# Moving five branch prefetch hints from the last five units of a kernel to a place ahead of its third batch

## The chip, the cores and the metric

The kernel runs on one core of one Trainium2 chip. The metric is the device time of one execution in microseconds, as the median over several runs. A hardware profile of one execution stands beside it: for every instruction its engine, start and duration, the semaphores it waits for, and every DMA packet with its queue. The core has five engines that each run a stream of instructions of their own: PE (matrix products), DVE (vector), ACT (activation), POOL (general) and SP (which here issues DMAs and closes the program). Their instructions themselves arrive by DMA, in packets that the profile counts under the kind "instruction".

## What is computed

An attention over 8 batches of 8 heads, with 576 tokens and 16 beacon keys of width 64, feeds a low-rank mixer over the tokens and a two-layer network over the channels:

```python
k_all = np.concatenate([beacon_k, k], axis=2)            # 16 + 576 keys
v_all = np.concatenate([beacon_v, v], axis=2)
scores = (q @ k_all.transpose(0, 1, 3, 2)) / sqrt(64)    # causal over the 576 tokens
a = softmax(scores)
x = (a @ v_all).transpose(0, 2, 1, 3).reshape(8, 576, 512)
h = x.transpose(0, 2, 1) @ U @ V                         # rank 32, over the tokens
u = x + h.transpose(0, 2, 1)
out = u + maximum(u @ w_ch1, 0) @ w_ch2                  # 512 -> 2048 -> 512
```

## The kernel before

The work is one unrolled program with no loop on its main path. A pair of heads is a visit (32 in all, four a batch): scores (L410), exponentials on ACT (L419), masks on DVE (L349), the product with the values (L428) and the division by the row sums (L436, L437). After a batch's four visits its mixer runs, and the tokens of all batches are then taken in nine blocks of 512 through the two layers. These blocks are cut into "units", small functions in a list named `queue`, and `fill(n)` runs the next n of them between pieces of the attention, so that PE always has something to do. The order of all five engines is written out by hand (`manual_schedule`): a line of code that comes earlier stands earlier in each engine's stream.

The main path takes exponentials without subtracting the row's maximum. At the end it tests whether any row sum left a safe range: `guard` and `guard_sum` put one number into `badi`, and `values_load` reads it into a register of every engine (L1577). If the number is not zero, a general path computes everything again in a loop over the batches (`with tc.If(n_bad != 0, label="general")`, L1631). For the data here it is zero, and every engine jumps over the general path to the end of the program. The jump is one compare-and-branch an engine, in the profile under L1631. The program's closing semaphores stand under L1676.

A branch can be announced by a hint instruction, one an engine. `tc.mark_branch_hint_location("general", engines=[...])` puts the five hints where it is called, inside a `tc.block()`, and each names the engine's own branch at the label "general". In the profile they are `BRANCH_PREFETCH_HINT` at L1676.

```python
        fill(len(queue) - 8)
        n_bad = nc.values_load(badi[0:1, 0:1], min_val=0, max_val=P)
        fill(len(queue) - HINT)                     # HINT = 5
        with tc.block():
            tc.mark_branch_hint_location("general", engines=[ENG.PE, ENG.Activation, ENG.DVE, ENG.SP, ENG.Pool])
            fill(len(queue))
            hold_back()
```

`hold_back` is a short chain of one-element operations (DVE L1106, ACT L1107, DVE L1108, PE L1110, ACT L1112) that keeps PE, ACT and DVE from the branch until DVE's last addition is done. Ahead of it stand the last additions of the output (L849), the products that they wait for (L909) and the stores of the last block (L858, on SP and ACT).

The third batch is the first one whose visits the loop `for p in range(NP1, NP)` plays. Ahead of that loop the second batch's mixer and its units run, with the regrouping of the third batch's keys and queries on DVE (L292, L294), their transposes on PE (L299), and second-layer products of the first block (L1053).

Of the kernel before, what the change touches and what calls it, by code (L numbers as in the profile page):

```python
# [16 lines left out]
ENG = mybir.EngineType  # L17
# [13 lines left out]
def kernel(  # L31
# [75 lines left out]
    def pst(shape, dtype, name):  # L107

        b = emptied.pop(0)
        t = psum.tile(shape, dtype, tag=f"bank{b}", name=name)  # L110
        bank_of[id(t)] = (b, t)
        return t

    def emptying(t):
        emptied.append(bank_of.pop(id(t))[0])
# [465 lines left out]
    def quad_tiles(q):  # L581

        if q == 0:
            w = [pairs.tile([P, 512], F16, name=f"lw{k}", tag=f"pr{k % 2}") for k in range(4)]
        else:
            w = [staged[q - 1][:, ds(512 * k, 512)] for k in range(4)]
            f = staged[q + 1][:, 0 : 2048].bitcast(F32).rearrange("p (k i x) -> p k i x", k=2, i=2)
            lq["k", q] = (f[:, 0], f[:, 1], f[:, 0])
        lq["w", q] = [x.rearrange("p (c f) -> p c f", c=2) for x in w]
# [17 lines left out]
    def quad_weights(q):  # L607

        def part(c0, d):
            return w1[:, ds(c0, 2), ds(P * d, 2 * P)]  # L610

        a11, a12, a21, a22 = part(0, 2 * q), part(2, 2 * q), part(0, HF + 2 * q), part(2, HF + 2 * q)
        s1, s2, s3, s4 = lq["w", q]
        return [
            lambda o=o, x=x, y=y, op=op: nc.gpsimd.tensor_tensor(out=o, in0=x, in1=y, op=op)
            for o, x, y, op in (
                (s1, a21, a22, ALU.add), (s2, s1, a11, ALU.subtract),
                (s3, a11, a21, ALU.subtract), (s4, a12, s2, ALU.subtract),
            )
        ]  # L620
# [483 lines left out]
    def hold_back():  # L1104

        nc.vector.tensor_copy(out=bad[0:1, :], in_=ones[0:1, :])  # L1106
        nc.scalar.activation(out=warm[0:1, :], in_=bad[0:1, :], func=AF.Copy)  # L1107
        nc.vector.tensor_copy(out=bad[0:1, :], in_=warm[0:1, :])  # L1108
        bps = pst([1, 1], F32, name="bps")
        nc.tensor.matmul(bps, bad[0:1, :], ones[0:1, :], start=True, stop=True)  # L1110
        emptying(bps)
        nc.scalar.activation(out=warm[0:1, :], in_=bad[0:1, :], func=AF.Copy)  # L1112
# [7 lines left out]
    def load_batch(b):  # L1120
        if b < DT0:
            Ls[b] = qk_tiles(b)
            emit_loads(b, Ls[b], vss[b % 2])
        else:
            coming.append(lambda: v_beacon(beacon_v[b], vss[b % 2]))
            coming.extend(lambda j=j: v_tokens(v[b], vss[b % 2], ALLH, [j]) for j in range(NT))

    def load_whole(b):

        Ls[b] = qk_tiles(b)  # L1130
        for i, (src, m) in enumerate(((k[b], nk), (q[b], nq))):
            dst = Ls[b][1][i]
            if i == 0:
                coming.append(lambda d=dst: beacon_load(nc.gpsimd, beacon_k[b], d[:, 0, :, :], ALLH))
            for j in range(NT):
                coming.append(lambda d=dst, s=src, a=m[j] - nq[j], n=m[j], j=j: nc.gpsimd.dma_start(  # L1136
                    out=d[a:n, j, :, :], in_=s[:, ds(q0[j], nq[j]), :].rearrange("h p d -> p h d")
                ))
# [6 lines left out]
    def turns(b):  # L1145

        all_coming()
        new_qT(b)
        kn, qn = Ls[b][1]

        def keys(j0, n):
            nc.sync.dma_start_transpose(
                out=kTs[b % 2].rearrange("p c (j x) -> p (c j) x", x=P)[:, NH2 * j0 : NH2 * (j0 + n), 0 : nk[j0]],
                in_=kn[: nk[j0], j0 : j0 + n, :, :].rearrange("p j h d -> p (j h d)"),
            )

        def queries(j):
            nc.sync.dma_start_transpose(
                out=qTs[b][:, :, ds(q0[j], nq[j])], in_=qn[: nq[j], j, :, :].rearrange("p h d -> p (h d)")
            )  # L1160

        return [lambda: keys(0, NT - 1)] + [lambda j=j: queries(j) for j in range(NT)] + [lambda: keys(NT - 1, 1)]
# [54 lines left out]
    def qkT_of(p):  # L1217
        b, c = divmod(p, NH2)
        new_qT_of(p)
        copies = [(act_copy, nc.vector.tensor_copy) if p == 0 else (nc.vector.tensor_copy,)] * 2  # L1220
        if p in ACT_KEYS:
            copies[0] = (act_copy,)
        if p == NP1:
            copies[1] = (act_copy,)
        turns = by_heads(Ls[b][0], c)
        for i, t in enumerate(prs.get(p, ())):
            if t is not None:
                turns[i] = in_pair(prs[p])[i]
        return qkT_units(turns, qTs[b], kTs[b % 2], c, copies, Ls[0][0][0] if p == 0 else None)
# [11 lines left out]
    def av_of(p):  # L1241
        b, c = divmod(p, NH2)
        if c == 0:
            assert not coming or b < DT0
            xbs[b] = xbp.tile([P, NT, DM], F16, name="xb", tag="xb")
        return [
            lambda i=i: av_unit(b, 2 * c + i, expts_of(p)[i], vss[b % 2], xbs[b]) for i in range(2)
        ]
# [7 lines left out]

    DT0 = 4
    LAG = 10
    HINT = 5
    FAST = 1  # L1260
    PARTS = {3: 1, 4: 1, 5: 1, 6: 3, 7: 3, 8: 3}
    AHEAD = 10
# [8 lines left out]
    queue = []  # L1271
    state = {"t": 0}

    def fill_turns(tr, n):
        for u in tr[:n]:
            u()
        del tr[:n]

    def fill(n):
        while n > 0 and queue:  # L1280
            u = queue.pop(0)
            if u is not None:
                u()
            for x in storing:
                x[0] -= 1
            while storing and storing[0][0] < 0:
                storing.pop(0)[1]()
            if coming:
                coming.pop(0)()
            n -= 1  # L1290
# [46 lines left out]
    def play(line):  # L1337

        for word in line.split():
            what, p = word[0], int(word[1:].split(":")[0] or 0)  # L1340
            if what == "f":
                fill(1)
            elif what in "qk":
                qkT_of(p)["qk".index(what)]()
            elif what == "r":
                regroup_of(p)
            elif what in "ab":
                if what == "a":
                    avs[p] = av_of(p)
                avs[p]["ab".index(what)]()  # L1350
            elif what in "mno":
                units = scores_of(p)
                units[2]() if what == "m" else units[3]("no".index(what))
            elif what == "e":
                scores_of(p)[int(word[-1]) // 2]()
            elif what == "v":
                visit([(int(x[: x.index(":")]), int(g)) for x in word[1:].split(",") for g in x[x.index(":") + 1 :]])

    with tc.manual_schedule(engines={ENG.PE, ENG.Activation, ENG.DVE, ENG.SP, ENG.Pool}):
# [111 lines left out]
        def turn_x(b):  # L1471
            turn, head, parts = mix_units(xbs[b], S * b)
            turn()
            later_mix[:] = [head] + parts

        def mix_between(b):

            mixing[:] = later_mix
            feed(b)
# [69 lines left out]
        )  # L1549

        for p in range(NP1, NP):
            b, c = divmod(p, NH2)
            if c == (1 if b >= DT0 else 0) and b + 1 < B:
                load_batch(b + 1)
            if p == P6 + 3:
                quad_tiles(0)
                coming.extend(quad_weights(0))
            if c == (1 if b + 1 == DT0 else 2) and DT0 <= b + 2 < B:
                load_whole(b + 2)
            qk = qkT_of(p + 2) if P6 <= p and p + 2 < min(NP, DT0 * NH2) else []  # L1560
            if p == P6:
                turn_x(b - 1)
                mix_between(b - 1)
            if c == 0 and DT0 <= b + 1 < B:
                tr = turns(b + 1)
                fill_turns(tr, len(tr))
            if p < P6:
                play(third[c])
            else:
                long_slot(p, c, av_of(p), qk or [lambda: None] * 2)  # L1570
# [4 lines left out]
        queue.insert(len(queue) - 14, guard_sum)  # L1575
        fill(len(queue) - 8)
        n_bad = nc.values_load(badi[0:1, 0:1], min_val=0, max_val=P)  # L1577
        fill(len(queue) - HINT)
        with tc.block():
            tc.mark_branch_hint_location("general", engines=[ENG.PE, ENG.Activation, ENG.DVE, ENG.SP, ENG.Pool])  # L1580
            fill(len(queue))
            hold_back()


    def safe_head(h, qT, kT, vs, xb):
# [95 lines left out]
```

## Time and profile before

| what | value |
| --- | --- |
| time, median of 3 runs | 333.34 us (333.2 to 333.98) |
| the profiled execution's own time | 333.34 us |
| its span, first to last instruction | 331.6 us |
| busy share of the span | PE 97%, PEld (weight loads) 69%, DVE 80%, ACT 59%, POOL 50% |
| granted PE clock | 1.000 |
| packets of instructions | q8: 30 (0.49 MB), q14: 19 (0.16 MB) |

In the profile's rows a `q` behind an engine's name (DVEq, PEldq) means its sequencer: branches, semaphore waits and hints, which are not counted as busy. A row such as `x14: 17/28/2051` gives a count and the shortest, median and longest duration in ns. The chain of work goes back from the last instruction that did work, at each step to what released it.

### The profile page before, as it was taken

The page shows a single profiled execution, that of the slowest core. Times are in us where ns is not written, and L with a number is a line of the kernel's source. Part 1 is how long each engine was busy: PE and PEld are TensorE (multiplying, and loading weights), DVE is VectorE, ACT ScalarE, POOL GpSimd, SP SyncE. Part 2 cuts the span into 40 slices and gives each one's busy share as a digit, 9 for nine tenths or more (in the row PEclk, how much of TensorE's full clock was granted, in tenths as well). Part 3 has the DMA queues.
Part 4 walks back from the last instruction along what each step waited for, and adds up shares of the span by engine and source line. Part 5 has one row for each costly group of instructions (what it writes and reads, how often), then busy time and mean ns, then how long its engine had stood idle before and what let it go on. Part 6 is the DMA issues. An engine that isn't in the chain of part 4 may idle for free.

```text
span 331.6 us, 9286 instructions
## 1 busy us (share of the span) xinstructions
PE 323.0 (97%) x3661; PEld 228.2 (69%) x3661; DVE 264.2 (80%) x610; ACT 196.9 (59%) x432; POOL 166.8 (50%) x263
## 2 busy tenths in 40 slices
PE   7899999999999999999999999999999999999993
PEld 3564555555578656876688888764887888788783
DVE  6676988668998668786878777877788898798993
ACT  5967961689972677348844795479536614704700
POOL 8976744658238960689058923940283036030030
PEclk9999999999999999999999999999999999999999
DMA  8999999999999996899999998995014313305003
GB/s 167 136 165 148 176 187 201 195 193 160 98 129 166 213 133 105 101 171 135 152 149 165 153 135 135 114 203 87 4 65 129 62 43 113 51 30 163 3 30 104
DMA packets 150561, 41.99 MB, mean 127 GB/s; under 512 B 131312, under 2 KB 149936, under 8 KB 150512
## 3 DMA queue, kind: packets, MB, share of 16 engines
q0 software_dynamic: 87568, 18.18, 72.6%
q1 hardware_dynamic: 62144, 22.41, 36.8%
q10 hardware_dynamic: 800, 0.75, 0.7%
q8 instruction: 30, 0.49, 0.6%
q14 instruction: 19, 0.16, 0.2%
HBM read 37.45 MB, written 9.44 MB: 141 GB/s over the span
## 4 chain that ended last, share of the span: by engine, by line
PE 92%; ACT 4%; DMA 2%; DVE 1%; ACTq 0%; issue 0%
PE gps L675 21%; PE po L428 9%; PE mpsA L909 9%; PE qpsA L701 6%; PE mpsD L829 6%; PE sps L410 6%; PE cps L1053 4%; PE gps L1027 4%; PE mpsE L829 3%; PE mpsC L829 3%; PE mpsB L829 3%; PE qpsD L701 3%; PE mpsF L829 2%; ACT expt L377 2%; ACT w L377 2%; PE tps L299 2%
## 5 line engine op out<-in xcount | busy, mean ns | idle before, releaser
L577 POOL TENSOR_TENSOR ob<-ob,ut 128x128 f32<-128x128 f32 x104 | 50.0, 511 | 121.7 <-DVE ob L849 59.4
L419 ACT ACTIVATE expt<-sps 128x496 f16<-128x496 f32 (+2 forms) x192 | 82.0, 542 | 41.8 <-PE sps L410 41.8
L675 PE MATMUL gps<-uT,w 128*128 128x512 f16 (+1 forms) x368 | 78.1, 352 | 0.0
L829 PEld LDWEIGHTS <-gT 128*128 128x128 f16 x576 | 54.3, 98 | 8.7 <-issue 2.6
L675 PEld LDWEIGHTS <-w 128*128 128x128 f16 x368 | 33.2, 98 | 25.6 <-issue 1.6
L653 DVE TENSOR_TENSOR gT<-gT 128x1024 f16<-128x1024 f16 (+3 forms) x87 | 47.0, 561 | 0.9
L683 ACT ACTIVATE gT<-gps 128x512 f16<-128x512 f32 x63 | 37.5, 619 | 16.1 <-PE gps L675 11.9
L239 POOL DMA_DIRECT2D vs<-in_v_dram x50 | 40.0, 811 | 13.9 <-DMA w<-in_moe_w_ch_dram 10.8
L428 PEld LDWEIGHTS <-expt 128*128 128x128 f16 x900 | 33.9, 98 | 8.4 <-issue 1.5
L428 PE MATMUL po<-vs,expt 128*128 128x65 f16 x900 | 36.4, 194 | 0.6 <-DVE expt L349 0.4
L909 PEld LDWEIGHTS <-gT 128*128 128x128 f16 x336 | 31.1, 98 | 4.0
L437 DVE TENSOR_TENSOR xb<-po,rec 128x320 f16<-128x320 f32 x64 | 31.4, 491 | 2.2
L349 DVE TENSOR_TENSOR expt<-expt,bigmask 128x768 f16<-128x768 f16 x56 | 31.3, 598 | 0.4 <-ACT expt L419 0.2
L720 ACT ACTIVATE kept<-qpsA 128x512 f32<-128x512 f32 x18 | 10.9, 603 | 24.1 <-PE qpsA L701 13.2
L410 PE MATMUL sps<-qT,kT 64*128 64x80 f16 (+4 forms) x288 | 22.6, 281 | 0.0
L436 DVE RECIPROCAL rec<-po 128x5 f32<-128x5 f32 x64 | 11.9, 186 | 12.8 <-PE po L428 12.5
L377 ACT ACTIVATE expt<-sps 128x496 f16<-128x496 f32 (+2 forms) x48 | 20.7, 589 | 0.7 <-PE sps L371 0.6
L909 PE MATMUL mpsA<-w,gT 128*128 128x256 f16 x160 | 19.1, 273 | 0.0
L410 PEld LDWEIGHTS <-kT 64*128 64x128 f16 x288 | 10.2, 94 | 12.8 <-issue 8.2
L681 DVE TENSOR_SCALAR gT<-gps 128x512 f16<-128x512 f32 x17 | 11.7, 689 | 8.8 <-PE gps L675 8.6
L1136 POOL DMA_DIRECT2D st<-in_k_dram x20 | 16.9, 860 | 1.3 <-DVE pr L294 1.3
L1136 POOL DMA_DIRECT2D st<-in_q_dram x20 | 16.9, 869 | 1.0 <-DMA st<-in_k_dram 0.5
(165 smaller groups left out, 540.4 us busy)
## 6 DMA issues: line engine op xcount, KB each, us to landing
out_dram<-ob SPq DMA_DIRECT2D x33, 256.0 KB, 3.2
vs<-in_v_dram POOLq DMA_DIRECT2D x18, 128.0 KB, 7.0
w<-in_moe_w_ch_dram POOLq DMA_DIRECT2D x4, 512.0 KB, 7.1
w<-in_moe_w_ch_dram POOLq DMA_DIRECT2D x2, 1024.0 KB, 12.2
st<-in_k_dram POOLq DMA_DIRECT2D x12, 128.0 KB, 6.2
st<-in_q_dram POOLq DMA_DIRECT2D x12, 128.0 KB, 7.8
st<-in_k_dram POOLq DMA_DIRECT2D x4, 288.0 KB, 11.7
st<-in_q_dram POOLq DMA_DIRECT2D x4, 288.0 KB, 12.4
```

The costliest lines, as they stand in the source:

```text
L239: nc.gpsimd.dma_start(out=dst[a : a + nq[j], j, :, :], in_=src[hs, ds(q0[j], nq[j]), :].rearrange("h p d -> p h d"))
L377: nc.scalar.activation(out=ex[i][:, ds(AT[g], gw[g])], in_=ps[g, i][:, 0 : gw[g]], func=AF.Exp, scale=scale)
L410: nc.tensor.matmul(banks[i][:, ds(at0 + o, w)], kT(hp, c, ch), qT[hp, c, ds(qa, w)], start=True, stop=True, skip_group_check=len(unit) > 1,)
L419: nc.scalar.activation(out=at[p][3][i][:, ds(AT[g], gw[g])], in_=bank[:, ds(at0, gw[g])], func=AF.Exp, scale=scale)
L428: nc.tensor.matmul(po[:, j, :], ex[0 : nk[c], ds(blk[(c, j)], P)], vs[0 : nk[c], ds(c * H * E + h * E, E)], start=(c == 0), stop=(c == j),)
L577: nc.gpsimd.tensor_tensor(out=o[:, i, ds(c, w)], in0=x[:, i, ds(c, w)], in1=y[:, i, ds(c, w)], op=op)
L653: nc.vector.tensor_tensor(out=o[:, ds(d0, n)], in0=x[:, ds(d0, n)], in1=y[:, ds(d0, n)], op=op)
L675: nc.tensor.matmul(g[:, ds(o, w)], w1[:, cc, ts(dc, P)], uT[:, cc, ds(at, w)], start=(cc == 0 and o == 0), stop=(cc == NCC - 1), skip_grou ...
L683: nc.scalar.activation(out=cell["g"][:, dc, :], in_=g, func=AF.Relu)
L829: nc.tensor.matmul(ps, a()[:, d, ds(P * i, P)], bm[:, d, ds(c0, w)], start=fresh and d == 0 and i == 0, stop=d == HF - 1, skip_group_check ...
L909: nc.tensor.matmul(ps, a()[:, d, ds(P * i, P)], bm[:, d, ds(c0, w)], start=fresh and d == 0, stop=d == HF - 1, skip_group_check=True,)
L1136: coming.append(lambda d=dst, s=src, a=m[j] - nq[j], n=m[j], j=j: nc.gpsimd.dma_start(out=d[a:n, j, :, :], in_=s[:, ds(q0[j], nq[j]), :].r ...
```

## The change

The constant `HINT` goes. The block around the hints holds nothing else any more and stands ahead of the loop over the later visits; the last units and `hold_back` follow `values_load` without a block.

```diff
-    HINT = 5
...
+        with tc.block():
+            tc.mark_branch_hint_location("general", engines=[ENG.PE, ENG.Activation, ENG.DVE, ENG.SP, ENG.Pool])
+
         for p in range(NP1, NP):
...
         n_bad = nc.values_load(badi[0:1, 0:1], min_val=0, max_val=P)
-        fill(len(queue) - HINT)
-        with tc.block():
-            tc.mark_branch_hint_location("general", engines=[ENG.PE, ENG.Activation, ENG.DVE, ENG.SP, ENG.Pool])
-            fill(len(queue))
-            hold_back()
+        fill(len(queue))
+        hold_back()
```

In the instruction streams the hints move and nothing changes places with them, except that POOL's stream gets one more row ahead of its first `ob` addition (L577), a select of its library. The unconditional branches that a block brings lead to the next instruction; in the trace of before no such row was run. Lines below the change count one less afterwards (L1676 is then L1675).

On DVE, at the end of the main path, before:

```order
L849 TENSOR_TENSOR ob<-mpsD,ob 128x128 x2
L1579 UNCONDITIONAL_BRANCH
L1676 BRANCH_PREFETCH_HINT
L849 TENSOR_TENSOR ob<-mpsA,ut 128x256 x2
L849 TENSOR_TENSOR ob<-mpsD,ob 128x256
L849 TENSOR_TENSOR ob<-mpsD,ob 128x128 x2
L1106 COPY bad<-ones 1x1
L1108 COPY bad<-warm 1x1
L1579 UNCONDITIONAL_BRANCH
L1631 COMPARE_AND_BRANCH
```

The hint stands seven operations ahead of the branch it is for, ten rows with the waits. After the change this place reads:

```order
L849 TENSOR_TENSOR ob<-mpsD,ob 128x128 x2
L849 TENSOR_TENSOR ob<-mpsA,ut 128x256 x2
L849 TENSOR_TENSOR ob<-mpsD,ob 128x256
L849 TENSOR_TENSOR ob<-mpsD,ob 128x128 x2
L1106 COPY bad<-ones 1x1
L1108 COPY bad<-warm 1x1
L1630 COMPARE_AND_BRANCH
```

The hint and the block's branches are gone, the additions and the branch stay. DVE's hint is now among the regrouping copies ahead of the third batch (`pr` is the regrouped tile, `st` the staged input):

```order
L294 COPY pr_1393<-st_113 16x128
L292 COPY pr_1396<-st_114 96x768
L1550 UNCONDITIONAL_BRANCH
L1675 BRANCH_PREFETCH_HINT
L1550 UNCONDITIONAL_BRANCH
L292 COPY pr_1442<-st_113 96x768
L294 COPY pr_1442<-st_113 16x128
```

It stands between two visits' copies. On PE the hint is now between the second layer's products of the first block (`cps`) and the next transposes (`tps`):

```order
L1053 LDWEIGHTS gT
L1053 MATMUL cps<-w_94,gT 128x512
L1550 UNCONDITIONAL_BRANCH
L1675 BRANCH_PREFETCH_HINT
L1550 UNCONDITIONAL_BRANCH
L299 LDWEIGHTS pr_1396
L299 MATMUL tps<-ident,pr_1396 128x96
```

Before, PE's hint stood between two products `mpsA` (L909) of the last block, some 80 instructions ahead of its branch.

## The prediction

> **What bounds the kernel now.** I read the page first, then the chain that ended last, then the rows of the last ten microseconds by line, then the queue's waits, and at the end the instruction packets by stretch.
>
> ```profile
> span 331.6 us, 9286 instructions
> PE 323.0 (97%) x3661; PEld 228.2 (69%) x3661; DVE 264.2 (80%) x610; ACT 196.9 (59%) x432; POOL 166.8 (50%) x263
> ...
> PE 92%; ACT 4%; DMA 2%; DVE 1%; ACTq 0%; issue 0%
> ```
>
> PE is busy for 97% of the span and carries 92% of the chain. A change that adds or takes no arithmetic can therefore pay in two places only: where PE would stand still, and in the tail after PE's last product. The chain's end shows where that tail begins.
>
> ```profile
> 319.43 1.77 PE mpsD L909 x24
> 321.19 3.51 PE mpsA L909 x32
> ...
> 325.18 1.70 DMA out_dram<-ob
> ...
> 327.28 0.20 ACT warm L1112
> ```
>
> The last row of engine work starts at 327.28 and takes 0.20, yet the span is 331.6. The last 4.1 us hold no arithmetic at all. What fills them is seen in the rows of the branch (L1631) and of the program's end (L1676), where the hints also stand. The columns are line, engine, operation, count, then duration in ns as minimum/median/maximum, then the first and the last start in us.
>
> ```profile
> L1631 DVEq COMPARE_BRANCH  x1: 84/84/84, 327.1 to 327.1; - x1
> L1631 SPq COMPARE_BRANCH  x1: 72/72/72, 327.2 to 327.2; - x1
> L1631 ACTq COMPARE_BRANCH  x1: 68/68/68, 327.3 to 327.3; - x1
> L1631 PEldq COMPARE_BRANCH  x1: 388/388/388, 327.3 to 327.3; - x1
> L1631 SPq EVENT_SEMAPHORE  x5: 17/17/17, 327.4 to 327.8; - x5
> L1631 PEldq EVENT_SEMAPHORE  x1: 51/51/51, 327.7 to 327.7; - x1
> L1631 ACTq EVENT_SEMAPHORE  x1: 17/17/17, 327.8 to 327.8; - x1
> L1631 DVEq EVENT_SEMAPHORE  x1: 21/21/21, 330.5 to 330.5; - x1
> ...
> L1676 SPq EVENT_SEMAPHORE  x14: 17/28/2051, 327.8 to 331.6; - x14
> L1676 PEldq BRANCH_PREFETCH_HINT  x1: 45/45/45, 320.9 to 320.9; - x1
> L1676 DVEq BRANCH_PREFETCH_HINT  x1: 51/51/51, 323.5 to 323.5; - x1
> L1676 SPq BRANCH_PREFETCH_HINT  x1: 65/65/65, 323.5 to 323.5; - x1
> L1676 ACTq BRANCH_PREFETCH_HINT  x1: 55/55/55, 324.4 to 324.4; - x1
> L1676 POOLq BRANCH_PREFETCH_HINT  x1: 55/55/55, 319.2 to 319.2; - x1
> SPq L1676 <- DVEq L1631: 2.1, 1, 2.1
> ```
>
> Four engines branch within 0.2 us of each other. From the branch to the next instruction behind it SP needs 0.2 us, PE 0.4, ACT 0.5. DVE needs 3.4 (327.1 to 330.5). The last row, from the queue's waits, says who pays: SP, which closes the program, stands 2.1 us for DVE, one of its fourteen waits of otherwise 28 ns (the 2051 in the row above). So the tail ends with DVE's jump, and that is what I price.
>
> Why is DVE alone slow? The packets of kind "instruction" tell it. Four stretches, in this order: up to 319 us, 320.9 to 323.4 (PE's hint and 2.5 us behind it), 323.4 to 328 (the other hints and all four branches), 328 to 329.
>
> ```profile
> q8 instruction: 28, 0.46, 0.6%
> q14 instruction: 15, 0.12, 0.1%
> ...
> q8 instruction: 1, 0.02, 2.4%
> ...
> DMA packets 1044, 0.81 MB, mean 176 GB/s; under 512 B 125, under 2 KB 1044, under 8 KB 1044
> q10 hardware_dynamic: 576, 0.46, 30.4%
> q1 hardware_dynamic: 468, 0.35, 23.4%
> ...
> q8 instruction: 1, 0.02, 8.1%
> q14 instruction: 2, 0.02, 6.8%
> ```
>
> Up to 319 us q8 brings 28 packets of 0.46 MB / 28 = 16 KB, and PE alone has some 7,000 instructions by then, so q8 is PE's and a packet is about 260 of its instructions (7,322 in all by the page). q14 brings 15 packets of 8 KB for the other four. Behind PE's hint comes one q8 packet, and PE's jump is short. Between 323.4 and 328 all 1,044 packets are of q10 and q1 (576 + 468), none is an instruction packet: DVE's hint at 323.5 fetched nothing, and its target came only after the branch, in 328 to 329. In the order of the instructions ACT, POOL and SP have under 100 rows between the branch and the end, within about one packet of where they already are. DVE has some 390 rows and PE some 1,230. Only these two jump far enough to need a fetch, PE's hint gets it and DVE's does not.
>
> **The change part by part.**
>
> *DVE's hint, the one that matters.* It goes from ten rows ahead of the branch to 65 us, some 520 of DVE's instructions or four packets earlier. Its worth hangs on one thing the trace cannot show outright: whether a hint is kept until the branch's part of the program comes near, or is spent at once. For kept: in the program a hint names its branch, and DVE's, ten rows of some 130 to a packet ahead of it, did nothing at all at 323.5, most likely because DVE was already inside the packet that holds the branch. This is what a fetch rule gives that looks at the hint when the branch's packet comes up in turn. PE's hint stood some 80 instructions ahead, a third of a packet, so its branch may well have lain in a packet that PE had not yet entered. Against: PE's packet came within 2.5 us of its hint, as if at once. The bounds are the rows of the branch: at best DVE jumps as ACT does (0.5 us, no gain on the path beyond SP's wait), at worst it needs 3.4 again. I take the best end, because silence at DVE and success at PE fit one rule only when the hint acts as its branch's packet comes in. The gain: DVE would be through at 327.1 + 0.5 = 327.6, SP reaches its wait at about 328.5 (330.6 less 2.1), 0.9 us later, so the wait falls whole from 2.05 to 0.03 us: -2.02 us. Next late are SP's own fourteen semaphore rows, which stay.
>
> *PE's hint.* Moved 5,700 PE instructions, some 22 packets, ahead. Kept: its jump stays 0.4 us, 0. Lost: rival 1.
>
> *ACT's, SP's and POOL's hints.* Their targets are in without a packet, so early or late they change nothing: 0.
>
> *The hint rows themselves.* Five of 45 to 65 ns, 271 ns in all, leave the tail and stand at the place ahead of the third batch. In the tail they cost nothing now: PE's chain rows abut (319.43 + 1.77 = 321.20) across PE's hint at 320.9, and the stores behind ACT's and SP's hints wait for DVE. The new places are seen in the timeline (start, duration, engine and line): PE's ahead of the first row, DVE's ahead of the second, SP's between the two stores of the third.
>
> ```profile
> 65.84 0.42 PE L299 MATMUL tps<-ident,pr 96*128 96x96 f16 x6
> ...
> 65.79 0.19 DVE L294 COPY pr<-st 16x128 f16<-16x128 f16 x1
> ...
> 65.07 6.80 SPq L1070 DMA_DIRECT2D out_dram<-ob  x2
> ```
>
> SP idles between its two stores, and PE runs from a filled queue as in the tail. Lower bound -0.1 (ACT's and DVE's rows, if they did delay the last store), upper +0.27 (nothing hidden); I take 0, since PE showed no gap at its own. The waits of all rows are the same in both orders, and the block opened around the hints has no rows of its own in the trace of before (no row of L1579 ran), so no queue stops there; POOL's hint falls between two load issues and adds its 55 ns to them at most.
>
> *POOL's new row.* The order has one row more on POOL, a library select at L577 ahead of the first `ob` addition. Its nearest rows are these:
>
> ```profile
> masks.py:199 POOLq MODIFY_POOL_CONFIG  x2: 37/37/37, 2.3 to 2.3; - x2
> ...
> L577 POOL TENSOR_TENSOR ob<-ob,ut x104: 414/428/971, 99.9 to 320.9; 128x128 f32<-128x128 f32 x104
> L577 POOLq EVENT_SEMAPHORE  x28: 17/43/7466, 92.3 to 302.9; - x28
> ```
>
> The same select at the start shows as two rows of 37 ns, and at the new place it stands ahead of POOL's 7,466 ns wait at 92.3 us, so even a hundred times 37 ns would be covered: 0.
>
> Sum: 333.34 (this execution, which is also the median of the three; 331.6 of span and 1.7 around it) - 2.02 = 331.3 us. Its own range is 331.0 to 331.7: below, the hints' 0.1 and 0.2 of scatter; above, a jump of DVE that still takes 1.8 us, through at 328.9 and so 0.4 after SP's arrival.
>
> **The rivals.**
>
> *1. An early hint is spent at once, and what it fetched is overwritten by the packets that follow.* DVE then misses as now, and PE misses too. PE's miss is bounded below by DVE's 3.4 us (327.3 + 3.4 = 330.7), and its packet is longer: 8.1% of 16 engines for 1 us is 1.30 us against 6.8% / 2 = 0.54 for one of q14, 0.8 more, 331.5. SP's wait then ends 0.2 to 1.0 us later than now: 333.5 to 334.3, taken as 334.0. For it: PE's packet came at once. The same time comes out if DVE gains and PE alone loses, for SP waits for both. [...]
>
> *2. The hint is kept for PE but never works on DVE.* Then only a row of 45 to 65 ns moves: 333.3. For it: the one hint of DVE that was run fetched nothing. Against: ten rows ahead is an extreme place.
>
> *3. Slower: the early fetch takes the place of the next packet in turn.* In the run of before no engine had to go on past its packet after the hint; at 65 us all must. PE would come to the end of its packet within 319 / 28 = 11.4 us, find the next one gone, stand there for a DVE-like 3.4 us less the 0.4 of a jump that hits, plus up to 0.8 for the larger packet, 3.0 to 3.8, nearly all of it on a 97% engine, and then lose as in rival 1: 333.34 + 3.4 + 0.7 = 337.4. It decides if PE is idle over 2 us there. Against: q8 brought packet upon packet without a gap beside the chain, and a hint that breaks the line after it would be of little use anywhere.
>
> **How the numbers follow.** Forecast 0.55, rival 1 (with its half) 0.20, rival 2 0.13, rival 3 0.12. About 0.3%, 1.0 us, is what three runs can tell from no change. Faster: the forecast, 0.55. Within it: rival 2 and most of rival 1 (333.5 to 334.3), 0.13 + 0.14 = 0.27. Slower: the rest of rival 1 and rival 3, 0.06 + 0.12 = 0.18. The range for 8 in 10 goes from 330.9 to 334.4 and leaves out rival 3 and the top of rival 1.
>
> **What would show it.** Right: DVE's semaphore row behind its branch at about 327.6, no L1676 wait over 0.3 us on SP, an instruction packet of q14 for DVE well ahead of 327, a span of about 329.6, and no new PE gap between 60 and 80 us. Rival 1 shows PE's row behind the branch at 330.7 or later and a q8 packet after it; rival 3 an idle PE within 11 us behind its hint; POOL's new row is wrong if POOL is late for `ob` at 99.9 us. The forecast fails if the packets of q8 and q14 come right behind the early hints and DVE's jump is still 3.4 us.

## The result, and the profile after

The changed kernel takes 331.22 us (median of 7 runs, 331.03 to 331.68) against 333.34 (7 runs, 332.69 to 334.83): a ratio of 0.9933, 95% interval 0.9914 to 0.9951. The prediction was 331.3. The profiled execution took 331.11 us. The page gives its span and, among the queues, the instruction packets (count, MB, share of 16 engines):

```profile
span 329.4 us, 9288 instructions
...
q8 instruction: 29, 0.48, 0.6%
q14 instruction: 17, 0.14, 0.2%
```

Before there were 30 and 19. So the early hints brought no packet on top; three fewer move. The rows of the branch, now L1630, show what became of the jumps:

```profile
L1630 DVEq COMPARE_BRANCH  x1: 84/84/84, 326.9 to 326.9; - x1
L1630 SPq COMPARE_BRANCH  x1: 72/72/72, 327.0 to 327.0; - x1
...
L1630 PEldq COMPARE_BRANCH  x1: 388/388/388, 327.1 to 327.1; - x1
L1630 DVEq EVENT_SEMAPHORE  x1: 21/21/21, 327.5 to 327.5; - x1
L1630 PEldq EVENT_SEMAPHORE  x1: 51/51/51, 327.6 to 327.6; - x1
```

DVE's next row comes 0.6 us behind its branch (before: 3.4), PE's jump reads 388 ns as before. In the rows of the program's end, now L1675, SP has no long wait left, and the five hints stand at 57 to 65 us:

```profile
L1675 SPq EVENT_SEMAPHORE  x14: 17/28/28, 327.6 to 329.4; - x14
...
L1675 POOLq BRANCH_PREFETCH_HINT  x1: 59/59/59, 56.8 to 56.8; - x1
L1675 DVEq BRANCH_PREFETCH_HINT  x1: 51/51/51, 63.2 to 63.2; - x1
L1675 PEldq BRANCH_PREFETCH_HINT  x1: 45/45/45, 64.2 to 64.2; - x1
L1675 ACTq BRANCH_PREFETCH_HINT  x1: 55/55/55, 65.0 to 65.0; - x1
L1675 SPq BRANCH_PREFETCH_HINT  x1: 60/60/60, 65.3 to 65.3; - x1
```

The span is 2.2 us shorter. 2.02 of it is SP's wait (2,051 to 28 ns). The other 0.2 is that this execution came to the branch 0.2 us earlier (DVE's at 326.9 instead of 327.1), which is less than the seven times of one kernel differ among themselves. What SP still waits for in the last 3 us, from the queue's waits (us in total, times, longest), has no DVE in it:

```profile
SPq L1675 <- PEq L1675: 0.7, 2, 0.5
...
SPq L1675 <- DMA out_dram<-ob: 0.2, 1, 0.2
```

Two more views answer the rivals. The first lists the queues from 59 to 74 us, a stretch that holds the hints of DVE, PE, ACT and SP and the 9 us behind them; the second is the busy time by stretch (the stretch's ends and length, then PE, PEld, DVE, ACT and POOL, each with its instructions, then clock, DMA share and GB/s).

```profile
DMA packets 9707, 2.93 MB, mean 195 GB/s; under 512 B 7786, under 2 KB 9323, under 8 KB 9707
...
q0 software_dynamic: 9275, 2.14, 191.6%
q1 hardware_dynamic: 432, 0.79, 17.5%
```

```profile
60.00:70.00 10.00, 10.00 (x96) 5.09 (x94) 5.61 (x13) 7.93 (x20) 7.23 (x10) 1.00 1.81 216
70.00:80.00 10.00, 10.00 (x121) 5.58 (x118) 8.44 (x22) 9.02 (x22) 7.34 (x9) 1.00 2.74 154
```

9,275 + 432 = 9,707: not one of the packets in the first stretch is an instruction packet, so none of these four hints was spent at once. PE is busy for all of the 20 us around and behind them.

### The profile page after: what moved, and what is told of

Same layout as the page of the kernel before. It is cut to its first block, busy times and chain, and to the rows that moved or that the text cites. A ratio compares the mean times of both kernels' runs of the same rounds, so it can differ in the third digit from the quotient of the medians.

```text
span 329.4 us, 9288 instructions
## 1 busy us (share of the span) xinstructions
PE 323.4 (98%) x3661; PEld 228.6 (69%) x3661; DVE 263.6 (80%) x610; ACT 196.8 (60%) x432; POOL 167.2 (51%) x263
## 4 chain that ended last, share of the span: by engine, by line
PE 93%; ACT 4%; DVE 1%; DMA 1%; issue 0%
PE gps L675 22%; PE po L428 9%; PE mpsA L909 9%; PE qpsA L701 6%; PE mpsD L829 6%; PE sps L410 6%; PE cps L1053 4%; PE gps L1027 4%; PE mpsE L829 3%; PE mpsC L829 3%; PE mpsB L829 3%; PE qpsD L701 3%; ACT expt L377 2%; PE mpsF L829 2%; ACT w L377 2%; PE mpsD L909 2%
## 5 line engine op out<-in xcount | busy, mean ns | idle before, releaser
L577 POOL TENSOR_TENSOR ob<-ob,ut 128x128 f32<-128x128 f32 x104 | 50.0, 511 | 120.7 <-DVE ob L849 59.4
L909 PEld LDWEIGHTS <-gT 128*128 128x128 f16 x336 | 31.2, 98 | 3.9
L909 PE MATMUL mpsA<-w,gT 128*128 128x256 f16 x160 | 19.1, 273 | 0.0
```

Of the source, the lines that this page charges most:

```text
L577: nc.gpsimd.tensor_tensor(out=o[:, i, ds(c, w)], in0=x[:, i, ds(c, w)], in1=y[:, i, ds(c, w)], op=op)
L909: nc.tensor.matmul(ps, a()[:, d, ds(P * i, P)], bm[:, d, ds(c0, w)], start=fresh and d == 0, stop=d == HF - 1, skip_group_check=True,)
```

## The experiments

All are variants of the changed kernel. Experiments 1, 2, 3 and 6 ran beside the kernel before at 333.13 us (median of 32), experiments 4, 5, 7 and 8 beside it at 332.97 (median of 35). The times above 335 us in experiments 3 to 8 (17 executions) have 5.0 to 5.7 us outside their span, from first to last instruction, where 1.6 to 1.8 is usual. What causes this is open, so in these experiments the spans are read beside the times.

**1. DVE's hint alone is early.** The other four go back to the last five units.

```diff
-            tc.mark_branch_hint_location("general", engines=[ENG.PE, ENG.Activation, ENG.DVE, ENG.SP, ENG.Pool])
+            tc.mark_branch_hint_location("general", engines=[ENG.DVE])
...
-        fill(len(queue))
+        fill(len(queue) - 5)
+        with tc.block():
+            tc.mark_branch_hint_location("general", engines=[ENG.PE, ENG.Activation, ENG.SP, ENG.Pool])
+        fill(len(queue))
```

> Only DVE's hint stands ahead of the third batch; the other four stand in the last five units as before. Theory (a hint is kept, and the packet with its target comes in the turn of the packet that follows the branch's): DVE's jump takes 0.4 to 0.6 us, SP's longest wait at the end is 28 ns, 331.2 us like the changed kernel, and q8 shows 30 packets again, since PE's late hint fetches out of turn. Rival (the gain came from PE's hint or from the emptier tail): 332.3 to 333.4 us.

Measured: 331.27 us (331.01 to 332.29), ratio 0.994 (0.9921 to 0.996). The rows of its program end:

```profile
L1678 SPq EVENT_SEMAPHORE  x14: 17/28/28, 327.7 to 329.5; - x14
...
L1678 DVEq BRANCH_PREFETCH_HINT  x1: 56/56/56, 63.3 to 63.3; - x1
...
L1678 PEldq BRANCH_PREFETCH_HINT  x1: 45/45/45, 320.8 to 320.8; - x1
```

DVE's hint alone gives the whole gain; moving the other four is worth nothing that this measurement can tell. Between 311 and 327 us this kernel has two q8 packets, the one in turn and the one 1.1 us behind PE's late hint:

```profile
q8 instruction: 2, 0.03, 0.9%
q14 instruction: 1, 0.01, 0.2%
```

The changed kernel has one q8 packet in the same stretch:

```profile
q8 instruction: 1, 0.02, 0.4%
q14 instruction: 1, 0.01, 0.2%
```

One packet less, and PE's jump is still short (388 ns; 482 in experiment 1). Up to there both kernels have the same 28 q8 packets, so PE's early hint added none here. That the packet in turn at 311.6 brought the jump's target is the author's inference; no row shows what a packet holds.

**2. No hints.** The block with the hints is left out.

```diff
-        with tc.block():
-            tc.mark_branch_hint_location("general", engines=[ENG.PE, ENG.Activation, ENG.DVE, ENG.SP, ENG.Pool])
```

> The five hints of the jump are left out. Theory: DVE and PE both miss, ACT, SP and POOL do not. DVE's jump takes 3.4 us as in the kernel before; PE's takes 3.4 to 4.2 us, since its packet is twice as long, and the time is that of rival 1 of the prediction, 333.5 to 334.3 us. Rival (PE's target comes in without a hint, or PE's miss is no longer than DVE's): 333.3 us.

Measured: 333.83 us (333.68 to 335.14), ratio 1.0011 (0.9989 to 1.0033). Its branch rows:

```profile
L1627 PEldq COMPARE_BRANCH  x1: 3731/3731/3731, 327.2 to 327.2; - x1
L1627 ACTq EVENT_SEMAPHORE  x1: 17/17/17, 327.6 to 327.6; - x1
L1627 DVEq EVENT_SEMAPHORE  x1: 21/21/21, 330.3 to 330.3; - x1
L1627 PEldq EVENT_SEMAPHORE  x1: 51/51/51, 331.0 to 331.0; - x1
```

This is what rival 1 would have looked like: PE's jump takes 3.7 us, DVE's 3.3, ACT's is as short as with a hint (327.2 to 327.6 us, in the changed kernel 327.1 to 327.6). The medians stand 0.70 us apart, though the interval still holds no difference. It has one q8 packet from 311 to 327 us, as the changed kernel has, so a packet comes there without any hint too; behind it PE's jump took 3.7 us here and 0.4 in the changed kernel.

**3. DVE's hint 56 instructions ahead, the others early.** It becomes a unit of the work queue.

```diff
+        def hint_unit():
+            with tc.block():
+                tc.mark_branch_hint_location("general", engines=[ENG.DVE])
+
+        queue.insert(len(queue) - 28, hint_unit)
```

> DVE's hint stands 56 instructions ahead of its branch, by count inside the packet that holds the branch, some 20 us ahead of it; the other four are early. Theory as the prediction put it (a hint acts only when the branch's packet comes in): too late, DVE's jump takes 3.4 us and the time is 333.3 us. Rival (a hint acts at once inside the branch's packet too, and the ten instructions or the 3.7 us of the kernel before were only too few): a q14 packet 1 to 2 us behind the hint, a jump of 0.5 us, 331.2 us.

Measured: 333.31 us (332.96 to 336.68), ratio 1.0011 (0.9989 to 1.0033).

```profile
L1680 SPq EVENT_SEMAPHORE  x14: 17/28/2086, 327.8 to 331.6; - x14
...
L1680 DVEq BRANCH_PREFETCH_HINT  x1: 56/56/56, 305.5 to 305.5; - x1
```

SP waits 2.1 us for DVE again, whose next row comes 3.5 us behind its branch (327.1 to 330.6). In the kernel before the hint came 3.7 us ahead, only just more than the 3.4 that DVE's jump took; here it comes 21.7 us ahead, and the jump is no shorter. Between these two runs it is not a matter of time left.

**4 and 5. The hint on either side of the place where DVE is taken to enter the branch's packet.** The author's estimate for it is some 115 instructions ahead of the branch, where DVE stands at about 279 us: q14 brings a packet at 279.5 us in the kernel before and at 279.3 in the changed kernel, there the only one from 270 to 300 us. The edit is that of experiment 3 with 64 in place of 28 (122 instructions ahead), and with 56 (107 ahead).

> DVE's hint stands 122 instructions ahead of its branch, seven rows ahead of the place where DVE enters the packet that holds the branch (row 576 by the fetches of the runs so far, about 279 us); the other four hints stand early. Theory (a hint counts when the packet behind the branch's own is fetched in turn, just after DVE enters the branch's packet): the hint is in time, the instruction packet at about 280 us brings the target, DVE's branch takes 0.6 us, no packet of 8 KB right behind DVE's branch; 331.2 us (331.0 to 331.7). Rival (only a hint far ahead, as the 534 rows of the changed kernel, is in time): DVE's branch takes 3.4 us, 333.3 us.

> The same hint 15 instructions later, 107 ahead of the branch and eight rows behind the packet's entry, so some 2 us behind the fetch; still over 40 us ahead of the branch. Theory: too late, DVE's branch takes 3.4 us and the time is that of the kernel before, 333.2 us (332.9 to 333.7). Rival (what counts is the distance or the time that is left to fetch): it does as well as 122 ahead, 331.2 us.

Measured: 122 ahead 331.35 us (331.11 to 335.37), ratio 0.9969 (0.9941 to 0.9997); 107 ahead 333.11 us (332.79 to 336.51), ratio 1.001 (0.999 to 1.0029). DVE's first row behind its branch (L1635) and the program's end, of the one and then of the other:

```profile
L1635 DVEq EVENT_SEMAPHORE  x1: 21/21/21, 328.6 to 328.6; - x1
...
L1680 SPq EVENT_SEMAPHORE  x14: 17/28/28, 328.7 to 330.4; - x14
...
L1680 DVEq BRANCH_PREFETCH_HINT  x1: 51/51/51, 275.8 to 275.8; - x1
```

```profile
L1635 DVEq EVENT_SEMAPHORE  x1: 21/21/21, 330.1 to 330.1; - x1
...
L1680 SPq EVENT_SEMAPHORE  x14: 17/28/1618, 327.8 to 331.1; - x14
...
L1680 DVEq BRANCH_PREFETCH_HINT  x1: 51/51/51, 281.5 to 281.5; - x1
```

Fifteen instructions decide here. DVE branches at 328.0 us in the first and at 327.1 in the second, so its jump takes 0.6 and 3.0 us. The instruction packet of q14 starts at 280.4 us in the first, 4.6 us behind the hint, and at 279.5 in the second, 2.0 us ahead of it. Each kernel has this one packet from 275 to 281.5 us; only in the first is DVE's jump short. No row says whose packet it is, since the page has only two queues of instructions, q8 and q14, for five engines. That it is DVE's is an inference from its place, some 115 rows ahead of the branch where a packet of 8 KB holds some 130 by the prediction's estimate, and from DVE's jump of 0.6 and 3.0 us on either side of it. Behind DVE's branch q14 brings two packets in the first (329.26 and 329.42 us) and three in the second (328.11, 328.33 and 330.66): the first of the three comes 1.05 us behind the branch, as in the kernel before (1.04), and the last 0.6 us behind DVE's next row.

The first profiled execution was late from early on: it reached PE's hint at 65.3 us, where the changed kernel reached it at 64.2, and PE's last product 1.06 us later. The second took 336.51 us, though its span is 331.1. The medians decide.

**6 and 7. PE's hint 19 instructions ahead, the others early,** run twice because the first profiled execution was already 1.4 us late at PE's last product.

```diff
-        fill(len(queue))
+        fill(len(queue) - 1)
+        with tc.block():
+            tc.mark_branch_hint_location("general", engines=[ENG.PE])
+        fill(len(queue))
```

> PE's hint alone stands 19 instructions ahead of its branch; the other four are early. In the kernel before PE's stood about 84 ahead and fetched at once. Theory of too little room (a hint needs several us or some tens of instructions to its branch): PE now misses, its jump takes 3.4 to 4.2 us, and the time is 331.2 + 2.1 to 2.9 = 333.3 to 334.1 us. Rival (PE acts on a hint at once wherever it stands): a q8 packet about 1 us behind the hint, which then comes in during the jump at worst, so 331.2 to 332.5 us.

> The kernel with PE's hint 19 instructions ahead of its branch, once more, since its first profiled execution was already 1.4 us late at PE's last matmul. Theory: PE acts on the hint at once, its packet of 16 KB moves while ACT and SP issue the last two stores, and lengthens these (1018 in place of 338 ns and 571 in place of 332 in the first run), which put 0.57 us between PE's last matmul and DVE's branch: 331.8 to 332.1 us where the start is not late, with ACT's last store issue again near 1 us. Rival: the long store issue was chance like the late start: 331.2 us with issues of 0.34 us.

Measured: 333.88 us (331.96 to 337.89), ratio 1.001 (0.9984 to 1.0037), then 333.17 (331.75 to 337.86), ratio 0.9985 (0.9961 to 1.0009). PE's jump is short in both:

```profile
L1633 PEldq COMPARE_BRANCH  x1: 527/527/527, 329.1 to 329.1; - x1
```

```profile
L1633 PEldq COMPARE_BRANCH  x1: 502/502/502, 327.7 to 327.7; - x1
```

A q8 packet starts 1.1 to 1.2 us behind the hint, and the jump of 527 and 502 ns stands against 3,731 without hints. So PE's hint worked in both runs 19 instructions ahead, by the prediction's estimate of 260 to a packet most likely inside the branch's own. The time is lost elsewhere. The issues of the last three stores, in the second run:

```profile
L858 SPq DMA_DIRECT2D out_dram<-ob x2: 344/508/673, 325.8 to 326.6; - x2
L858 ACTq DMA_DIRECT2D out_dram<-ob x1: 1118/1118/1118, 326.1 to 326.1; - x1
...
DMA to landing us min/median/max: 2.3/2.8/2.9
```

The same rows of the changed kernel:

```profile
L858 SPq DMA_DIRECT2D out_dram<-ob x2: 332/338/344, 325.9 to 326.6; - x2
L858 ACTq DMA_DIRECT2D out_dram<-ob x1: 338/338/338, 326.2 to 326.2; - x1
...
DMA to landing us min/median/max: 1.6/1.6/1.8
```

ACT's issue takes 1,118 in place of 338 ns, SP's last one 673 in place of 332. DVE waits for ACT's next operation (L1108 for L1107, 0.3 us in the changed kernel), so from the start of PE's last product to DVE's branch it is 1.55 us in place of 0.88. PE's packet ran from 325.26 to 326.83 and ACT's issue ended at 327.23, 0.40 us behind it; in the first run the packet ended at 328.20 and the issue at 328.60, again 0.40. Not every issue in the packet's time was long: SP's at 325.80, the first behind the packet's start, took 344 ns. The span of this execution is 0.96 us longer than the changed kernel's: 0.67 in that stretch and 0.35 behind DVE's branch, less 0.06 at the start.

The lowest time, 331.75, is 0.72 above the changed kernel's lowest, but most executions lose more: of the 24 spans, 10 lie at 330.1 to 330.9 us and 14 at 331.7 to 332.8. One of the 14 was profiled (experiment 6). It came to DVE's early hint at 64.6 us in place of 63.2, so its 1.4 us were lost long before PE's hint. Whether that holds for the others, and why there are so many, stays open.

**8. Without `hold_back`.** The six small operations ahead of the branch, whose values no output needs, are left out.

```diff
         fill(len(queue))
-        hold_back()
```

> The changed kernel without hold_back, the six small operations on DVE, ACT and PE ahead of the branch (they compute nothing that the output needs). Theory: with DVE's jump at 0.6 us the end is SP's row of semaphore waits behind its own last store, so what DVE, ACT and PE do some 0.3 us earlier is worth nothing: 331.2 us (330.9 to 331.5), SP's waits at the program's end all near 28 ns. Rival: the branches of PE and DVE come 0.3 to 0.7 us earlier, and so the packets that follow the jump fall on the last stores, whose issue they lengthen: 331.6 to 332.0 us, and SP's or ACT's last store issue reads over 0.5 us in place of 0.33.

Measured: 333.37 us (332.44 to 336.89), ratio 1.0042 (1.0008 to 1.0077).

```profile
L858 SPq DMA_DIRECT2D out_dram<-ob x2: 345/913/1481, 326.7 to 327.5; - x2
...
DMA to landing us min/median/max: 3.0/3.3/3.4
```

The theory (worth nothing) fell; the rival named what was then seen, a packet across the last store and a long issue, with too low a price. PE now branches at 325.9 (in the changed kernel at 327.1), and a q8 packet runs from 327.02 to 328.61, across SP's last store, whose issue takes 1,481 ns and ends at 328.99, 0.38 behind the packet. The stores then land 3.0 to 3.4 us after their issue (in the changed kernel 1.6 to 1.8). The span is 2.5 us longer than the changed kernel's: 0.9 because this execution came later to PE's last product (0.87 of it already at DVE's hint at 64 us), 1.15 from the start of that product to SP's branch (2.11 in place of 0.96), and 0.42 from SP's branch to the end (2.84 in place of 2.42). The median of the times overstates the price, since five of the twelve carry over 5 us outside the span; by the medians of the spans (331.2 against 329.5) it is 1.7 us.

No version beat the changed kernel.

## Why the prediction was right, point by point

- **The tail ends with DVE's jump: shown.** Experiment 1 moves DVE's hint alone and has the whole gain. The step said DVE through at 327.6 and 2.02 us off SP's wait; it was 327.5 and 2.02.
- **A hint is kept until its branch's packet is near: that an early hint still counts is shown, and for DVE now bracketed.** With DVE's hint at 63.2 us or 122 instructions ahead its jump took 0.6 us, 107 ahead 3.0, and a q14 packet starts between the two places (4.6 us behind the one hint, 2.0 us ahead of the other). By the author's estimate from its place, some 115 rows ahead of the branch where a packet holds some 130, DVE enters the branch's packet there, and the hint must have run before the packet that comes next, one later than the prediction had it; what that packet holds is not shown. The prediction's guess that DVE's late hint came inside the branch's packet agrees with this.
- **The same reason given for PE was wrong.** The prediction supposed that PE's late hint stood ahead of the branch's packet. But from 311 us to PE's branch at 327.1 and 327.2 q8 brings one packet in the changed kernel (at 311.6) and one without hints, so the late hint at 320.9 most likely lay inside the branch's packet already, and still a q8 packet started 1.1 us behind it. In experiments 6 and 7 one does so 19 instructions ahead too. So the silence at DVE and the success at PE do not fit one rule, as the step claimed; the choice of the best end stood on weaker ground than it says. That it held is in part luck: with early hints both engines had short jumps (0.6 and 0.4 us), which PE's late hint could not have shown. Why late hints went with jumps of 0.4 to 0.5 us on PE and of 3.0 to 3.5 on DVE was not tried and stays open.
- **PE's hint at 0: right.** 331.22 with PE's hint early, 331.27 with it in the last five units. It is 0 only there: 19 instructions ahead the kernel is slower, by 0.7 us in the lowest times.
- **ACT's, SP's and POOL's hints at 0: right.** ACT and SP reach the row behind their branch as soon without any hint (experiment 2: ACT 327.2 to 327.6 us, SP 327.1 to 327.3; changed kernel: 327.1 to 327.6 and 327.0 to 327.2). POOL comes to its branch at 319.1 us and reaches the row behind it at 321.6 in the changed kernel and at 321.7 without hints, both times right behind its last addition, so its jump is hidden either way. One q14 packet at 281.4 us is gone in the changed kernel; experiment 1, which gains as much, still has it, so it cost nothing. By the order of the rows it was SP's or POOL's, which is not shown.
- **The hint rows at 0: right,** within the 0.05 us between experiment 1 and the changed kernel; PE is busy for all of 60 to 80 us.
- **POOL's library select: the place and the cover right, the size too low.** It takes twice 74 ns and not 37, and still costs nothing: it falls inside POOL's wait of 7.4 us (92.2 to 99.6), behind which the first addition comes at 99.7 (before 99.9):

```profile
L577 POOL TENSOR_TENSOR ob<-ob,ut x104: 414/428/973, 99.7 to 320.7; 128x128 f32<-128x128 f32 x104
L577 POOLq EVENT_SEMAPHORE  x28: 17/43/7412, 92.2 to 302.7; - x28
L577 POOLq MODIFY_POOL_CONFIG  x2: 74/74/74, 94.2 to 94.3; - x2
```

- **Rival 1 (spent and overwritten) fell:** none of the 9,707 packets from 59 to 74 us, behind the early hints, is an instruction packet. Its price was sound: 334.0 expected, 333.83 measured with no hints at all.
- **Rival 2 (never works on DVE) fell** with experiments 1 and 4 (DVE's jump 0.6 us in both). **Rival 3 (the next packet is lost at once) fell:** PE shows no gap behind its hint (busy for all of 60 to 80 us), and the next q8 packet comes at 74.2 us (in the kernel before at 74.4).

## What to carry to other kernels

A hint close to its branch was worth nothing on one engine here and everything on another: with DVE's 10 to 107 instructions ahead its jump took 3.0 to 3.5 us, with PE's 19 to some 80 ahead 0.4 to 0.5. So read from the rows whether the engine's next row follows its branch in 0.5 or in 3.4 us, and place the hint a full packet ahead (here some 130 instructions on DVE, by the packets' sizes; 122 were enough) and not a few units. A jump that costs 3 us matters only if someone waits for that engine at the end; here SP waited 2.1 us for DVE's. And look where instruction packets fall among stores: here PE's packet among the last stores, behind a late hint or an early jump, went with 0.7 to 1.7 us more.

## What the runs showed of the hardware that was not expected

- An early hint still went with a short jump 264 us later on DVE (63.2 to 326.9 us, jump 0.6 us) and 263 us later on PE (64.2 to 327.1, 0.4), with 22 q8 packets between PE's hint and its branch and not one instruction packet from 59 to 74 us.
- With its hint 10, 56 and 107 instructions ahead (the 10 in the kernel before) DVE's jump took 3.4, 3.5 and 3.0 us. With PE's 19 and some 80 ahead a q8 packet started 1.1 to 1.2 us behind the hint, and PE's jump took 0.4 to 0.5 us.
- Beside a 16 KB instruction packet some issues were long: 1,018 and 1,118 ns on ACT in place of 338, 571, 673 and 1,481 on SP in place of 332, each ending about 0.4 us behind the packet, a little more than the length of an undisturbed issue. It isn't a matter of the program's end: SP's issue at 11.76 us (L191) took 1,492 ns in the kernel before and ended 0.38 us behind the packet of 11.82 to 12.87, and in the changed kernel the same issue, at 11.72, took 1,385 ns and ended 0.40 us behind the packet of 11.57 to 12.70. Other issues in a packet's time were not long (344 ns at 325.80 in experiment 7); what decides is open.
- `hold_back`, six operations of no use to the result, keeps PE's jump behind the last stores (PE branches at 327.1 us with it, 325.9 without) and is worth some 1.7 us (median span 329.5 us with it, 331.2 without).
